# One program order with per-item copy engines for a fused attention and mixing kernel, in place of a greedy order

## Chip, cores and metric

One NeuronCore of a Trainium2 chip. The metric is device time in microseconds (us) of one execution. Most executions of one kernel agree closely (the kernel before: 231.13 to 231.94 us in four); each has a mean granted TensorE clock and a state (fast or slow), and only fast runs are compared.

## The reference, cut to what matters

```python
# attention inside chunks of 64 tokens; B=8, H=8, S=576, D=64
scores = q_c @ k_c.T / sqrt(D);  attn = softmax(scores);  x = attn @ v_c
# mixing, per batch; x: [576, 512]
theta = x @ w_theta                       # 512 x 512
y = w_tok_r @ (x*cos(theta)) + w_tok_i @ (x*sin(theta))   # 576 x 576 each
u = x + y
out = u + relu(u @ w_ch)
```

## The kernel before

The eight batches are worked on in four pairs `p`. A pair has nine tiles of 128 tokens in five groups `g`; group 2 is the middle tile, half of it from each batch. The steps of TensorE are: `a1` transposes q and k, `a2` scores, `a3` attention times v, `a4` transposes x, `a5` theta, `tw` transposes the token weights, `y` mixes tokens, `w` is the last product. Each takes one of four buffers in PSUM (where this kernel's matmuls write), and copies on VectorE (DVE) or ScalarE (ACT) free it. The copies are called by what they write: qT, kT and xT are q, k and x transposed; `sin` and `cos` come from theta. Everything is emitted in program order, for each engine its own instructions.

```python
psum = ctx.enter_context(tc.tile_pool(name="psum", bufs=4, space=bass.MemoryType.PSUM))
def psum2(name, dtype=FP32):              # every step takes one of these four
    n = 1024 if dtype == FP32 else 2048
    return psum.tile([P, n], dtype, name=name, tag="ps")

def a1(p, g):
    ps = psum2("ps_qkT", FP16)
    ...                                   # 32 transposes
    nc.vector.tensor_copy(out=qT[...], in_=psv[:, 0, ...])
    nc.scalar.copy(out=kT[...].rearrange("p e s t -> p e t s"), in_=psv[:, 1, ...])

def a4(p, g):
    ...                                   # 4 transposes per tile
    if n == 2:
        nc.scalar.copy(out=xT[...], in_=psv)
        return
    nc.scalar.copy(out=xm, in_=psv)       # the middle tile
    for bb in range(2):
        nc.gpsimd.tensor_copy(out=xT[:, :, bb*S + KT*P : (bb+1)*S], in_=xm[:, :, bb*CH : bb*CH + CH])

# order: a greedy list scheduler with estimated durations picks the next step
od.segment([], front(0, B0) + tws + back(0, B0))          # B0 = groups 0, 2, 1
for p in range(NP):
    ...
    od.segment(main, back(p, B1), tail=4.0)               # main: y and w
    od.flush()
    if more:
        new_pair(p + 1)
        load_batch(p + 1, B0 + B1)                        # loads, issued from GpSimd
    ...
```

The softmax here doesn't subtract the row's maximum and nothing guards it: scores larger than these inputs give would overflow.

## Time and profile before

| | before |
|---|---|
| timed runs, median (range), 3 runs | 231.5 us (231.13 to 231.94) |
| the profiled run | 228.7 us, span 226.9, granted clock 0.995 |
| TensorE / VectorE / ScalarE / GpSimd busy | 201.7 / 120.2 / 130.5 / 88.5 us |
| first `ps_y` matmul starts; last matmul ends | 33.5; 222.6 us |

The lines behind this are in the prediction. In the rows of 40 slices a digit is a tenth of a slice's time. In a list of waits, "A <- B: 2.4, 3, 0.8" means that A waited 2.4 us in all, three times, at most 0.8, and that B came last. "issue" as a releaser means that the profile shows nothing that was waited for.

### The profile page before, as it was taken

The numbers are of one execution on the slowest core, as the hardware profiler recorded it, in microseconds if no ns is written. First come the engines' busy times: TensorE is split into PE (matmuls) and PEld (weight loads), VectorE is DVE, ScalarE is ACT, GpSimd is POOL, SyncE is SP. The second block draws the span as 40 slices with busy tenths as digits, with TensorE's granted clock in tenths as the row PEclk, the third lists the DMA queues.
The fourth block names the chain that finished last, engine by engine and source line by source line (L and its number), as shares of the span: only waits on it lengthen the run. The fifth ranks groups of instructions, "written<-read, shape, count | busy, mean of one in ns | idle before, by whom it ended". The sixth has DMA issues, their size and how long they took to land.

```text
span 226.9 us, 6743 instructions
## 1 busy us (share of the span) xinstructions
PE 201.7 (89%) x2994; PEld 140.3 (62%) x2994; DVE 120.2 (53%) x214; ACT 130.5 (58%) x151; POOL 88.5 (39%) x124
## 2 busy tenths in 40 slices
PE   0678979997898998999898998999898998999992
PEld 0564567855676656766785656666785657667751
DVE  0135373825547478446446477446456477356353
ACT  2355968357885881167785880267785880364142
POOL 8995487499100195981000295971000200000000
PEclk9999999999999999999999999999999999999998
DMA  6999999999920179999400189999200124013036
GB/s 63 165 156 186 192 180 187 144 124 168 222 22 3 48 102 197 221 168 208 129 3 3 49 118 225 195 169 222 99 3 3 49 69 139 3 46 139 2 110 217
DMA packets 83581, 26.93 MB, mean 119 GB/s; under 512 B 76256, under 2 KB 78944, under 8 KB 83552
## 3 DMA queue, kind: packets, MB, share of 16 engines
q0 software_dynamic: 77664, 16.54, 82.3%
q1 hardware_dynamic: 5888, 9.96, 12.6%
q8 instruction: 23, 0.38, 0.7%
q14 instruction: 6, 0.05, 0.1%
HBM read 33.06 MB, written 9.44 MB: 187 GB/s over the span
## 4 chain that ended last, share of the span: by engine, by line
PE 75%; ACT 14%; DVE 6%; DMA 2%; issue 1%; POOL 0%; DVEq 0%; ACTq 0%; POOLq 0%
PE ps_y L476 32%; PE ps_uw L496 13%; PE ps_theta L420 13%; ACT eT L342 5%; PE ps_qkT L307 5%; PE ps_sT L335 3%; PE ps_uw L503 3%; DMA qk<-in_k_dram 2%; PE ps_xT L391 2%; DVE uT L484 2%; DVE x L377 2%; ACT kT L317 2%; ACT cos L430 2%; ACT xT L398 2%; PE ps_x L363 2%
## 5 line engine op out<-in xcount | busy, mean ns | idle before, releaser
L476 PE MATMUL ps_y<-wT,z 128*128 128x288 f16 x512 | 68.2, 286 | 4.5 <-DVE x L377 2.4
L476 PEld LDWEIGHTS <-z 128*128 128x128 f16 x512 | 48.6, 98 | 18.5 <-DVE x L377 2.7
L246 POOL DMA_DIRECT2D v<-in_v_dram x56 | 42.1, 776 | 14.6 <-DMA qk<-in_k_dram 9.2
L484 DVE TENSOR_TENSOR uT<-ps_y,xT 128x576 f16<-128x576 f32 x32 | 24.2, 758 | 40.0 <-PE ps_y L476 40.0
L496 PE MATMUL ps_uw<-wch,uT 128*128 128x512 f16 x144 | 41.0, 379 | 2.3 <-ACT xT L398 1.7
L317 ACT COPY kT<-ps_qkT 128x1024 f16<-128x1024 f16 (+1 forms) x20 | 23.4, 1193 | 17.9 <-DVE qT L316 17.9
L404 POOL COPY xT<-xTm 128x256 f16<-128x256 f16 x8 | 4.9, 652 | 72.3 <-ACT xTm L402 72.3
L420 PE MATMUL ps_theta<-wtheta,xT 128*128 128x512 f16 x128 | 31.2, 388 | 1.7 <-ACT xT L398 1.7
L430 ACT ACTIVATE cos<-ps_theta,pihalf 128x1024 f16<-128x1024 f32 (+1 forms) x20 | 20.6, 1030 | 19.8 <-PE ps_theta L420 19.8
L503 PE MATMUL ps_uw<-id,uT 128*128 128x128 f16 x144 | 31.5, 219 | 0.0
L509 ACT ACTIVATE relu<-ps_uw 128x512 f32<-128x512 f32 x36 | 20.8, 603 | 18.4 <-PE ps_uw L503 18.4
L398 ACT COPY xT<-ps_xT 128x1024 f16<-128x1024 f16 x16 | 16.2, 1012 | 23.0 <-PE ps_xT L391 23.0
L515 DVE TENSOR_TENSOR o<-ps_uw,relu 128x512 f32<-128x512 f32 x36 | 24.0, 687 | 7.3 <-ACT relu L509 7.3
L307 PE MATMUL ps_qkT<-id,qk 128*64 128x128 f16 (+1 forms) x640 | 22.1, 227 | 6.4 <-DMA qk<-in_q_dram 5.8
L377 DVE TENSOR_TENSOR x<-ps_x,recip 128x512 f16<-128x512 f32 x36 | 24.9, 692 | 1.2
L307 PEld LDWEIGHTS <-qk 128*64 128x64 f16 (+1 forms) x640 | 18.9, 118 | 9.4 <-DMA qk<-in_q_dram 6.2
L316 DVE COPY qT<-ps_qkT 128x1024 f16<-128x1024 f16 (+1 forms) x20 | 12.6, 636 | 22.7 <-PE ps_qkT L307 22.7
L496 PEld LDWEIGHTS <-uT 128*128 128x128 f16 x144 | 14.1, 98 | 15.8
L420 PEld LDWEIGHTS <-xT 128*128 128x128 f16 x128 | 12.6, 100 | 15.7 <-ACT xT L398 2.1
L342 ACT ACTIVATE eT<-ps_sT 128x1024 f16<-128x1024 f32 (+1 forms) x20 | 18.3, 939 | 7.1 <-PE ps_sT L335 7.0
L443 DVE TENSOR_TENSOR z<-x,cos 128x1024 f16<-128x1024 f16 x16 | 11.1, 691 | 20.6 <-ACT cos L430 20.4
L225 POOL DMA_DIRECT2D qk<-in_k_dram x24 | 19.2, 804 | 3.6 <-DMA wch<-in_moe_w_ch_dram 1.6
(41 smaller groups left out, 199.1 us busy)
## 6 DMA issues: line engine op xcount, KB each, us to landing
out_dram<-o SPq DMA_DIRECT2D x32, 256.0 KB, 3.9
qk<-in_q_dram POOLq DMA_DIRECT2D x16, 256.0 KB, 6.4
qk<-in_k_dram POOLq DMA_DIRECT2D x16, 256.0 KB, 7.4
v<-in_v_dram POOLq DMA_DIRECT2D x40, 64.0 KB, 6.7
v<-in_v_dram POOLq DMA_DIRECT2D x16, 128.0 KB, 6.6
out_dram<-o SPq DMA_DIRECT2D x8, 128.0 KB, 4.1
wnat<-in_moe_w_tok_r_dram POOLq DMA_DIRECT2D x1, 576.0 KB, 9.9
wnat<-in_moe_w_tok_i_dram POOLq DMA_DIRECT2D x1, 576.0 KB, 11.9
```

The source lines that it names most:

```text
L246: nc.gpsimd.dma_start(v16[pp : pp + m, sl, :, 0:D], v[2 * p + bb, :, s0 : s0 + m, :].rearrange("h s d -> s h d"),)
L307: nc.tensor.transpose(psv[par * D : par * D + D, w, e, tk, 0:rows], t[0:rows, w, 2 * e + par, tk, :], id16[0:rows, 0:rows],)
L317: nc.scalar.copy(out=kT[:, :, 0:rows, :].rearrange("p e s t -> p e t s"), in_=psv[:, 1, :, :, 0:rows],)
L342: nc.scalar.activation(out=eT[:, 0:n].rearrange("p i e r c -> p r (i e) c"), in_=psv[:, :, 0:n].rearrange("p r i e c -> p r (i e) c"), fun ...
L377: nc.vector.tensor_tensor(out=xo, in0=px[:, :, :, 0:D], in1=recip.broadcast_to((P, 2, NE, D)), op=ALU.mult,)
L420: nc.tensor.matmul(ps[:, jj * DM : jj * DM + DM], xt[:, db, :], wtheta16[:, db, :], start=(db == 0), stop=(db == NDB - 1),)
L430: nc.scalar.activation(out=cos[:, 0:n].rearrange("p a e -> p (a e)"), in_=pin, func=AF.Sin, bias=pihalf, scale=1.0,)
L476: nc.tensor.matmul(psv[:, hf, 0:HS], z[:, db * P : db * P + P], wT[:, kt, hf * HS : hf * HS + HS], start=(kt == 0), stop=(kt == 2 * KT),)
L484: nc.vector.tensor_tensor(out=s["uT"][:, db, sl].rearrange("p (f c) -> p f c", f=2), in0=psv[:, :, 0:HS], in1=s["xT"][:, db, sl].rearrange ...
L496: nc.tensor.matmul(ps[:, 0:DM], uT[:, db, j * P : j * P + P], wch16[:, db, :], start=(db == 0), stop=(db == NDB - 1),)
L503: nc.tensor.matmul(ps[:, DM + db * P : DM + db * P + P], uT[:, db, j * P : j * P + P], id16,)
L515: nc.vector.tensor_tensor(out=o, in0=ps[:, DM : 2 * DM], in1=r, op=ALU.add)
```

## The change

The intent is to replace the greedy scheduler by a fixed order, found by annealing, that has no stalls on the four PSUM buffers. Each item carries flags for which engine copies. Groups are loaded and used in the order 0 to 4, x is held per group, the token weights come and are transposed in halves, and the middle tile's copy leaves GpSimd. The core of the diff, with cuts:

```diff
+ORDER = """
+a1.0.0:0 a2.0.0:0 a1.0.1:3 a3.0.0.0:0 a3.0.0.1:0 a2.0.1:0 a1.0.2:0 a3.0.1.0:0 a2.0.2:0
+a3.0.2.0:0 a4.0.2:3 a4.0.0:0 a3.0.1.1:0 a5.0.2:0 a4.0.1:1 z.0.2.0:0 a5.0.1:0 a5.0.0:0
+tw.1.2:0 z.0.0.0:0 z.0.0.1:0 tw.0.0:1 z.0.1.0:0 z.0.1.1:0 tw.1.1:1 tw.0.1:0 tw.0.2:0
+tw.1.0:1 a1.0.3:2 yh.0.0:0 a2.0.3:0 yh.0.1:0 ...            (cut)
-class Order: ...                                             (cut: the greedy scheduler)
+    def copy(eng, out, in_):
+        if eng: nc.vector.tensor_copy(out=out, in_=in_)
+        else:   nc.scalar.copy(out=out, in_=in_)
     def a1(p, g, bits):
-        nc.vector.tensor_copy(out=qT[...], in_=psv[:, 0, ...])
-        nc.scalar.copy(out=kT[...], in_=psv[:, 1, ...])
+        copy(not bits & 1, qT[...], psv[:, 0, ...])
+        copy(bits & 2, kT[...], psv[:, 1, ...])
     def a4(p, g, bits):
-        nc.scalar.copy(out=xm, in_=psv)
-        for bb in range(2):
-            nc.gpsimd.tensor_copy(out=xT[...], in_=xm[...])
+        copy(bits & 1, xm, psv)
+        copy(not bits & 2, xT.rearrange("p a (b s) -> p a b s", b=2)[:, :, :, KT*P : S],
+             xm.rearrange("p a (b s) -> p a b s", b=2))
+    # x16: one tile per group, bufs=6; before, one tile per pair, bufs=1
+    for item in ORDER:
+        ...                                # emit the step; then, as soon as a q/k buffer
+        load(loaded)                       # and a v slot are free in this order, the next load
```

## The prediction

> **What bounds the kernel now.** I read the page first (busy shares, the 40 slices, the chain), then the waits of TensorE and GpSimd, then the timeline of TensorE up to the first `ps_y`. From the page of the kernel before:
>
> ```profile
> span 226.9 us, 6743 instructions
> PE 201.7 (89%) x2994; PEld 140.3 (62%) x2994; DVE 120.2 (53%) x214; ACT 130.5 (58%) x151; POOL 88.5 (39%) x124
> ...
> PEclk9999999999999999999999999999999999999998
> DMA  6999999999920179999400189999200124013036
> ...
> PE 75%; ACT 14%; DVE 6%; DMA 2%; issue 1%; POOL 0%; DVEq 0%; ACTq 0%; POOLq 0%
> ```
>
> TensorE is the bound: 75% of the chain that ends last, at a full clock. VectorE and ScalarE are a little over half busy, and DMA works in bursts with long empty slices. But 89% busy is not 89% of what TensorE could do, so I count slots instead: how far one step's start lies from the next when nothing waits. These pieces of the chain in order of time (start, duration, what) give them:
>
> ```profile
> 89.09 0.25 PE ps_x L363 x16
> ...
> 91.66 0.45 PE ps_xT L391 x8
> ...
> 105.11 1.01 PE ps_qkT L307 x32
> ...
> 195.76 1.73 PE ps_theta L420 x8
> ...
> 206.21 6.62 PE ps_y L476 x54
> ```
>
> So `y` (18 matmuls) costs 6.62/3 = 2.21 us, 8 theta matmuls 1.73, 32 transposes of q and k 1.01, 8 of x 0.45, 16 attention matmuls 0.25. From the same views: scores 0.62 per 32, a small group's 32 transposes 0.63, `w` 1.08 (four pairs, 0.27 apart), 15 weight transposes 1.01. Whole kernel: y 32 x 2.21 = 70.7; w 36 x 1.08 = 38.9; theta 144 x 0.216 = 31.1; q and k 16 x 1.01 + 4 x 0.63 = 18.7; scores 18 x 0.62 = 11.2; attention 36 x 0.25 = 9.0; x 18 x 0.45 = 8.1; weights 50 x 0.067 = 3.4. Sum 191.1 us. The first matmul starts at 5.8 and the last ends at 222.6, 4.3 before the end (relu 0.60, add 0.69, store). So 216.8 - 191.1 = 25.7 us are lost between them. The first `ps_y` starts at 33.5; the work ahead of it is 15.3 us, so 33.5 - 5.8 - 15.3 = **12.4 us are lost in the opening** and (222.6 - 33.5) - 175.8 = **13.3 us after it**.
>
> TensorE's waits (line, releaser, us in total, times, longest) name them in part; the rest is restarts and stretches inside busy records:
>
> ```profile
> PE ps_y L476 <- DVE x L377: 2.4, 3, 0.8
> PE ps_sT L335 <- ACT kT L317: 2.1, 2, 1.1
> PE ps_uw L496 <- ACT xT L398: 1.7, 3, 0.6
> PE ps_theta L420 <- ACT xT L398: 1.7, 1, 1.7
> PE ps_y L476 <- ACT eT L342: 1.7, 2, 0.8
> ```
>
> `ps_y` needs neither `x` nor `eT` of the next group: it waits for one of the four PSUM buffers, freed by the copy named. So the steady loss is order: several short steps in a row, each leaving a copy of about 1 us, use up four buffers. GpSimd's waits:
>
> ```profile
> POOL xT L404 <- ACT xTm L402: 72.3, 3, 25.7
> ```
>
> The copies of the middle tile stand in the queue that issues the loads and hold it three times for some 25 us. After the first y no TensorE wait names a load, though, so this is hidden.
>
> [...] a `ps_y` matmul has a record of 286 ns but a slot of 2.21/18 = 123 ns. [...] the qT copy, 1024 elements, takes 690 ns, barely more than the 512-element f32 multiply's 692. The change puts kT, written at step 2, on VectorE, where no record of before exists[...]. [...]
>
> **The change part by part.** (1) *Matmuls.* I set the built order of both kernels side by side: the same 5990 rows on TensorE. The first batch's y is cut at 256 and 320 columns instead of 288 twice, the same total. No work goes; the floor stays 191.1. (2) *Table loads.* 10 before and 10 after: 0. (3) *Middle tile.* Eight GpSimd copies (4.9 us) go, four copies come: three on VectorE, one on ScalarE, below 0.6 us each. Off the path; what it buys is that loads are issued as the seven q/k buffers come free. (4) *Copies split.* Counting the order's flags: 9 kT move from ScalarE to VectorE, 6 qT the other way, about half of the xT copies to VectorE. ScalarE loses about 9 x 1.3 + 10 x 1.0 and gains 6 x 1.0: 130 to about 115. VectorE gains about 9 x 1.2 + 10 x 0.7 - 6 x 0.7: 120 to about 133. Both stay near 60%, below TensorE: worth time only where a buffer waited for the busier of the two. (5) *Opening.* Groups go 0, 1, 2, and the token weights are loaded and transposed in halves, but the order puts all six transposing steps ahead of the first y, and the first of them needs the last weight tail. In the trace that tail lands at about 27.8 (issued 16.7, 11.1 to landing); ScalarE then still has sin to 29.2 and three wT copies, two of 1280 elements. Walked by hand with these durations, the last wT copy y needs ends near 32.3 and the first y starts near 32.7: **0.8 us gained**, not the 12.4. (6) *Order after the opening.* The next pair's attention is spread thinly between y and w and x is held per group (six buffers). Walking the stretch from pair 0's `w` into its second half[...], every buffer is free at or just before its turn, with slack of 0.2 to 0.7 us. A real run won't hold that everywhere. My choice: **of the 13.3 us, 4.5 remain, 8.8 gained.** Sum: 0.8 + 8.8 = 9.6 us; span 226.9 - 9.6 = 217.3. The timed runs are 231.5 for a span of 226.9; I take the same microseconds off: **221.9, say 222.0 us**, 4.1% less.
>
> **The rivals.** *Loads become the bound.* Pairs 2 and 3 are transposed much earlier: by summed slots plus the opening, pair 2's first group at about 68 us and pair 3's at about 97, against 105 and 156 before. GpSimd issues a full group in 4.1 us (12.2 us for three from 45.2 to 57.4), landing about 7 later, so pair 2's group 0 lands near 65 and pair 1's group 1 near 47 against a need near 48.7. Slack is 2 to 4 us, and stores run beside it. If loads lag, TensorE stands 2 to 6 us between 45 and 80 us: 224 to 228. For it: slices at 9 in DMA up to 60 us. Against it: every delay elsewhere adds slack. *Four buffers still bind.* The slack of the walk is used up by longer copies (kT at 1.2 us)[...], so that 8 to 10 us stay: about 226. For it: PSUM still has four buffers and every step's copies are about as long. *The opening worsens*, by 1 to 3 us, because the weights come in six transfers instead of four and the first transposing step waits for the last of them, in front of everything: 223 to 225. *Everything holds*: 1 to 2 us lost after the opening, 218.5 to 219.5. [...]
>
> **Range and chances.** Gain if all holds 13, centre 9.6, with one rival 4 to 6, with two about 2. So 218.5 to 227.5 holds it 8 times in 10. Faster by over 2% means below 226.9: it needs only 4.6 of the 25.7 us; 0.85. Within 2%: two rivals together, 0.13. Slower: only if an order tuned to a model meets a load it did not foresee, 0.02.
>
> **What would show each step.** TensorE's sum of slots unchanged and its busy time lower than 201.7 by a few us (fewer restarts). The first `ps_y` at 32 to 33.5; if at 30 or at 35, step 5 is wrong. GpSimd never waiting for xTm, and the DMA row without its empty slices up to about 110 us. VectorE near 133 and ScalarE near 115 us busy, kT on VectorE near 1.2 us. Between the first y and the last matmul about 180 us instead of 189. A TensorE wait on q, k or v after 40 us would mean the first rival; a few us on VectorE or ScalarE copies ahead of y, w or the short steps, the second. The prediction is wrong above all if the 4.5 us is: nothing in the trace of before measures it.

## More of the kernel before

One line pair of the kernel before that I had looked at but not used is TensorE's timeline at its first theta (start, duration, engine, line, operation, how many):

```profile
21.38 2.85 PE L420 MATMUL ps_theta<-wtheta,xT 128*128 128x512 f16 x8
24.07 1.03 PE L420 MATMUL ps_theta<-wtheta,xTm 128*128 128x512 f16 x4
24.94 1.89 PE L420 MATMUL ps_theta<-wtheta,xT 128*128 128x512 f16 x8
```

The first eight matmuls take 24.07 - 21.38 = 2.7 us up to the next start, the last eight 1.7.

## The result, and the profile after

A ratio is the mean time of one kernel's fast runs over that of the other's of the same rounds, so it is not quite the ratio of the medians.

| | median (range), runs | ratio to before, 95% interval |
|---|---|---|
| before | 231.63 us (231.13 to 231.94), 4 | 1 |
| changed | 224.76 us (223.36 to 228.51), 4, one of them slow | 0.9685 (0.9623 to 0.9748) |
| changed (`after_again`) | 222.92 us (222.14 to 223.81), 4 | 0.9637 (0.9575 to 0.970) |

So it is 3.1 to 3.6% faster; 4.1% was predicted. The profile that came with the result fell in the slow state (clock 0.982), so I read `after_again`, the same kernel in the fast state. From its page:

```profile
span 221.7 us, 6717 instructions
PE 200.3 (90%) x2994; PEld 139.2 (63%) x2994; DVE 130.7 (59%) x230; ACT 117.4 (53%) x136; POOL 85.1 (38%) x118
...
PEclk9999999999999999999999999999999999999999
DMA  5999999999999999999990012112211211321236
...
PE 79%; DMA 10%; POOL 5%; issue 2%; ACT 1%; DVE 1%; ACTq 0%; POOLq 0%
```

The matmuls are the same 2994, VectorE and ScalarE have changed places, and the empty DMA slices before 115 us are gone. TensorE's waits after 45 us:

```profile
PE ps_sT L292 <- issue: 1.7, 2, 1.0
PE ps_sT L292 <- ACT kT L199: 0.6, 1, 0.6
PE ps_x L320 <- issue: 0.4, 1, 0.4
```

Of the list of before nothing is left but 0.6 us on one copy. In its place stand waits on nothing visible. Now the opening, from TensorE's timeline of the same run:

```profile
22.89 1.89 PE L377 MATMUL ps_theta<-wtheta,xTm 128*128 128x512 f16 x4
26.41 5.37 PE L377 MATMUL ps_theta<-wtheta,xT 128*128 128x512 f16 x16 [0.79 <-DVE xT L197]
...
37.09 1.05 PE L434 MATMUL ps_y<-wT,z 128*128 128x256 f16 x8
```

The first `ps_y` starts at 37.1, where before it started at 33.5. From there to the end of the last matmul it is 180.3 us instead of 189.1. So the part after the first y gained 8.8 us, and the opening lost 3.6.

There is a third term. The kernel before had granted clocks of 0.968 to 0.988 in the 25 runs timed beside the experiments, against 0.995 in its profiled run; all fast runs of the changed kernel had 0.996 to 1.000. The profiled run of before took 228.7 us, some 3 us less than its timed runs. So some 3 us of the timed difference seem to come with the clock, beside 5.2 us of span (226.9 to 221.7); that the clock is the reason was not shown.

### The profile page after: what moved, and what is told of

It is laid out like the page before. It is cut to its first block, busy times and chain, and to the rows that moved or that the text cites.

```text
span 226.4 us, 6717 instructions
## 1 busy us (share of the span) xinstructions
PE 203.6 (90%) x2994; PEld 140.9 (62%) x2994; DVE 130.9 (58%) x230; ACT 117.3 (52%) x136; POOL 85.1 (38%) x118
## 4 chain that ended last, share of the span: by engine, by line
PE 83%; ACT 6%; DVE 4%; issue 2%; DMA 2%; POOL 0%; ACTq 0%; POOLq 0%
PE ps_y L455 27%; PE ps_theta L377 16%; PE ps_uw L475 14%; PE ps_qkT L266 8%; PE ps_y L434 4%; PE ps_sT L292 4%; PE ps_xT L348 4%; PE ps_uw L482 4%; PE ps_x L320 3%; DMA qk<-in_k_dram 2%; ACT kT L199 2%; ACT eT L299 2%; DVE x L334 1%; DVE kT L197 1%; DVE qT L197 1%
## 5 line engine op out<-in xcount | busy, mean ns | idle before, releaser
L455 PE MATMUL ps_y<-wT,z 128*128 128x288 f16 x448 | 60.4, 289 | 0.0
L455 PEld LDWEIGHTS <-z 128*128 128x128 f16 x448 | 42.9, 99 | 13.3 <-issue 0.3
L475 PE MATMUL ps_uw<-wch,uT 128*128 128x512 f16 x144 | 43.5, 386 | 0.0
L463 DVE TENSOR_TENSOR uT<-ps_y,xT 128x576 f16<-128x576 f32 x28 | 21.2, 756 | 28.1 <-PE ps_y L455 28.0
L377 PE MATMUL ps_theta<-wtheta,xT 128*128 128x512 f16 x128 | 32.3, 400 | 0.8 <-DVE xT L197 0.8
L199 ACT COPY kT<-ps_qkT 128x1024 f16<-128x1024 f16 (+1 forms) x11 | 12.6, 1146 | 20.5 <-DVE qT L197 20.4
L155 POOL DMA_DIRECT2D qk<-in_q_dram x24 | 19.4, 813 | 1.4 <-POOLq L558 0.8
L391 ACT ACTIVATE sin<-ps_theta 128x1024 f16<-128x1024 f32 (+1 forms) x20 | 18.7, 935 | 0.0
L292 PE MATMUL ps_sT<-qT,kT 64*64 64x64 f16 x576 | 13.1, 224 | 5.2 <-ACT kT L199 3.3
L320 PE MATMUL ps_x<-v,eT 64*64 64x65 f16 x576 | 11.8, 202 | 4.1 <-issue 1.7
```

Of the source, the lines that this page charges most:

```text
L155: nc.gpsimd.dma_start(t[(pp // 2) : (pp // 2) + m // 2, ti].rearrange("p h t d -> p h (t d)"), src.rearrange("h (p t) d -> p h (t d)", t=2),)
L292: nc.tensor.matmul(psv[kh * CH : kh * CH + CH, par, i, e, :], kT[par * D : par * D + D, e, c0 : c0 + CH], qT[par * D : par * D + D, e, c0 ...
L377: nc.tensor.matmul(ps[:, jj * DM : jj * DM + DM], xt[:, db, :], wtheta16[:, db, :], start=(db == 0), stop=(db == NDB - 1),)
L455: nc.tensor.matmul(psv[:, hf, 0:HS], zt[:, db * P : db * P + P], wT[:, kt, hf * HS : hf * HS + HS], start=(kt == 0), stop=(kt == 2 * KT),)
L475: nc.tensor.matmul(ps[:, 0:DM], uT[:, db, j * P : j * P + P], wch16[:, db, :], start=(db == 0), stop=(db == NDB - 1),)
```

## The experiments

Twelve kernels ran.

**1. `after_again`: the changed kernel, unchanged.**

> The changed kernel unchanged, for a profile in the fast state. Both theories: 223 to 225.5 us, first ps_y at 36 to 37.5 us, theta matmuls in the opening at about 0.43 us from start to start (half speed) as in the first profile, and from the first y to the last matmul about 180 us. If the slow state alone had made the late opening, the first ps_y is here at 34 or below.

Measured: 222.92 us, first y at 37.1, 180.3 us after it.

**2. `open_before`: the opening put back.**

```diff
-a1.0.0:0 a2.0.0:0 a1.0.1:3 a3.0.0.0:0 ... a4.0.1:1 z.0.2.0:0 a5.0.1:0 a5.0.0:0
+a1.0.0:0 a1.0.2:0 a2.0.0:0 a2.0.2:0 a1.0.1:0 a3.0.0.0:0 a2.0.1:0 a3.0.0.1:0 a3.0.2.0:0
+a4.0.0:0 a3.0.1.0:0 a4.0.2:0 a3.0.1.1:0 a4.0.1:0 a5.0.0:0 a5.0.2:0 a5.0.1:0 z.0.2.0:0
+    LOADS[1], LOADS[2] = LOADS[2], LOADS[1]
```

> The changed kernel with the opening of pair 0 put back to the kernel before: loads and steps in the order 0, 2, 1 and no split of copies there, all that follows unchanged. Theory A (the new opening is a longer chain: two big groups first, qT on ScalarE and then kT on VectorE, and TensorE has more gaps): first ps_y at 33 to 34 us, total down 3 to 4 us, about 220.5. Rival B (the weights in six transfers instead of four delay the opening): first ps_y stays at 36 to 37, total within 1 us of the changed kernel.

Measured: first y at 33.6, as theory A expects, with the weights still in six transfers, so rival B falls. But the total is 222.33 us, only 0.6 below `after_again` (0.9 by the fast runs alone; one of its four was slow): a miss of some 3 us. From the first y to the last matmul it took 182.2 us instead of 180.3. The waits of this run that name no releaser:

```profile
PE ps_sT L292 <- issue: 3.0, 2, 1.8
...
PE ps_x L320 <- issue: 0.8, 1, 0.8
```

**3. `warm`: throw-away work in TensorE's gaps of the opening.**

```diff
+    warm = const.tile([P, 512], FP16, name="warm");  nc.vector.memset(warm, 0.5)
+    # into the PSUM buffer just taken, ahead of the step's own matmuls:
+    #   9 before the first step, 6 before a2.0.0, 5 before a3.0.0.0, 1 to 3 at five others,
+    #   10 transposes before a4.0.2
+    nc.tensor.matmul(ps[:, 0:512], warm[:, 0:P], warm)
```

> The changed kernel with throw-away matmuls and transposes in TensorE's gaps of the opening, written into the PSUM buffer of the next step ahead of its own work (results unchanged). Theory C [...]: theta matmuls in the opening at 0.22 us instead of 0.43, first ps_y at about 34, total down about 3 us. Theory A alone: theta slots get shorter but the chain of copies sets the first ps_y, at 36 or later, total down less than 1 us. If throw-away work does not speed TensorE up, slots stay at 0.43 and the total rises by up to 1 us.

The opening looks as theory C says:

```profile
22.68 1.04 PE L391 MATMUL ps_theta<-wtheta,xTm 128*128 128x512 f16 x4
...
25.09 3.63 PE L391 MATMUL ps_theta<-wtheta,xT 128*128 128x512 f16 x16
...
34.07 1.05 PE L448 MATMUL ps_y<-wT,z 128*128 128x256 f16 x8
```

Sixteen matmuls take 3.63 us instead of 5.37, and the first y starts at 34.1 instead of 37.1. Start to start they are 216 ns apart; in `after_again` they are 427 ns apart until 29.8 us and 216 from 30.1 on. One trace doesn't show that the throw-away work did it, though: `after_3`, `nosplit` and `pool_mid` have the changed kernel's opening without it, and their sixteen also ran at some 216 ns (first y at 35.0, 35.4 and 35.0). What only `warm` has is the short time in the first four too (1.04 us, in `after_again` 1.89); all five traces of this opening without throw-away work show those at 401 to 427 ns from start to start. Yet the total is 224.15 us, above `after_again`, with intervals that overlap. Again the part after the first y grew, to 182.7 us.

**4. `pool_mid`: the middle tile's copies back on GpSimd.** (The edit is the a4 part of the diff above, reversed.)

> The changed kernel with the middle tile's copies back on GpSimd. If in this order they stand behind the loads issued ahead of them (pair 1's first five groups, issued until about 55 us), pair 0's middle columns come only then, the additions of the first batch's second half wait, and the total rises by 8 to 15 us, to 232 to 239. If the move off GpSimd is worth nothing, within 1 us of the changed kernel.

Measured: 238.73 us, 15.8 more than `after_again` on the same chip. VectorE's longest wait after the first y, and TensorE's:

```profile
DVE uT L442 <- POOL xT L361: 15.1, 1, 15.1
...
PE ps_x L320 <- DVE uT L442: 11.6, 1, 11.6
```

The copies ran at 58.1 us, behind all loads issued ahead of them, and pair 0's first additions waited. Of the 15.8 us some 3 are more stops of the kind that comes next (6.0 us against 2.7). In this order the move off GpSimd is necessary, though in the old one it was worth nothing (experiment 5).

**What stops TensorE.** In experiments 1 to 3, TensorE stands in the middle of steps, where nothing is waited for. I numbered its records in the trace (weight loads, matmuls and its few sequencer records, in order of start, from 0). In `after_again` the gaps are before numbers 2241, 2753 and 3777; in `warm`, whose throw-away work shifts all numbers by 78, before 2241, 2497, 2753, 3009, 3777 and 4033. All are 193 modulo 256. The DMA part of the page has the other half:

```profile
q8 instruction: 23, 0.38, 0.7%
```

These are 23 packets of 16,384 bytes. If these 0.38 MB are the program of TensorE's 5990 instructions, one has some 63 bytes and a packet holds some 260: an estimate from these numbers, near the 256 of the gaps. The number of packets follows TensorE's instructions: 21 in `few_rows` with 5342, 24 in `warm` with 78 more. Ahead of each such gap one of them starts 2.2 to 2.8 us before TensorE goes on. So the reading is: TensorE has used up its program and waits for the next packet. Experiments 7, 9 and 12 test it. In the next table "stops" is the sum of the gaps over 0.4 us at these numbers, start to start, and the rest is what is left of the time from the first y to the end of the last matmul.

| kernel | first y | first y to last matmul | stops (how many) | rest |
|---|---|---|---|---|
| before | 33.5 | 189.1 | 0 | 189.1 |
| after_again | 37.1 | 180.3 | 2.7 (3) | 177.6 |
| after_3 | 35.0 | 180.8 | 3.2 (3) | 177.6 |
| open_before | 33.6 | 182.2 | 4.4 (3) | 177.8 |
| open_before_2 | 33.6 | 182.4 | 2.4 (2) | 180.0 |
| warm | 34.1 | 182.7 | 5.3 (6) | 177.4 |
| open_warm | 33.6 | 184.1 | 6.5 (5) | 177.6 |
| open_no_late_v | 34.1 | 183.2 | 4.8 (3) | 178.4 |
| few_rows | 34.1 | 178.3 | 0 | 178.3 |
| open_spread | 33.3 | 181.0 | 3.1 (3) | 177.9 |
| nosplit | 35.4 | 187.5 | 4.1 (3) | 183.4 |
| before_mid | 34.5 | 192.1 | 2.7 (2) | 189.4 |
| pool_mid | 35.0 | 198.1 | 6.0 (3) | 192.1 |

For nearly all kernels with the new order the rest is 177.4 to 178.4 us, against a floor of 175.8 by summed slots. The exception, `open_before_2`, had a granted clock of 0.93 between 66 and 90 us, right where its stops are.

**5. `before_mid`: the kernel before with one part of the change.** (Its a4 copies the middle tile with one `nc.vector.tensor_copy`.)

> The kernel before with one part of the change alone: the middle tile's copies on VectorE in one instruction instead of two on GpSimd, so that loads are no longer held up. If the loads are hidden in the old order, the time stays within 1 us of the kernel before although GpSimd never waits for xTm. If loads held it back, 2 us or more faster.

Measured: 233.41 us, ratio 1.0083 (1.0009 to 1.0157). GpSimd now waits for a free q/k buffer instead of for xTm:

```profile
POOL qk L225 <- PE ps_qkT L307: 15.7, 1, 15.7
```

The loads were hidden; this part alone gains nothing in the old order. The extra 1.3 us fit the two stops in its profile (which also has a granted clock of 0.50 from 32 to 36 us, in the opening); why they came here and not in the kernel before is answered under experiment 7.

**6. `nosplit`: every copy after the opening on its old engine, order unchanged.**

```diff
-tw.1.0:1 a1.0.3:2 yh.0.0:0 a2.0.3:0 yh.0.1:0 a1.0.4:2 ...   a4.0.4:1 ...
+tw.1.0:1 a1.0.3:0 yh.0.0:0 a2.0.3:0 yh.0.1:0 a1.0.4:0 ...   a4.0.4:0 ...
```

> The changed kernel with the split of the copies undone after the opening: qT on VectorE, kT and xT on ScalarE for every item, order unchanged. If the split matters because the four PSUM buffers are freed by whichever engine is less loaded, TensorE's waits on ScalarE copies grow and the total rises by 3 to 6 us. If the order alone does it, within 1 us.

Measured: 229.19 us, ratio to before 0.9878, where the changed kernel has 0.9637 and 0.9645: some 5.5 us. The rest column says the same, 183.4 instead of 177.6. TensorE's waits after 45 us show them coming back, apart from the stops:

```profile
PE ps_theta L377 <- ACT sin L391: 0.9, 1, 0.9
PE ps_uw L475 <- ACT sin L391: 0.9, 2, 0.6
PE ps_qkT L266 <- DVE o L494: 0.9, 1, 0.9
PE ps_xT L348 <- DVE o L494: 0.6, 1, 0.6
```

These steps don't read `sin` or `o`; they wait for the buffer that the reader held. The order was tuned together with the split, so 5.5 us is what the split is worth in this order, not a share that would add up.

**7. `open_no_late_v`: open_before without v's loads of pairs 2 and 3 (wrong values).**

```diff
     def load_v(p, g):
+        if p >= 2:
+            return
```

> open_before without the loads of v for pairs 2 and 3 (their results are wrong on purpose: old v is used). In open_before TensorE stands three times for 4.4 us in all in the middle of a step, waiting for nothing but its program; each stop is at an instruction number of 193 modulo 256[...]. If the program arrives late because the loads fill the DMA engines, with far fewer load packets between 60 and 105 us the first two stops shrink from 3.0 to under 1 us and the total falls by 2 us or more. If the stops come from how fast TensorE uses up instructions, they stay at 3 to 4.5 us, and the total within 1 us.

Measured: 224.32 us, stops of 4.8 us. That looks as if the theory "program late because loads fill the DMA engines" fell, but the run didn't empty the DMA engines where its three stops are. With v's loads gone, GpSimd issued those of q and k earlier. From TensorE's entry into each of the three stretches of 256 before these stops to the start of the next packet, `--windows` gives a DMA share of 1.55, 1.83 and 1.80, against 1.89, 1.95 and 1.35 in `open_before`. (The share sums the packets' times, so packets that overlap take it over 1.) Where the loads really were gone, the stop is gone too: the last load packet ended at 93.4 us instead of 115.1, and the stop before 3777 is missing. In `after_again`, too, that stop ends at 116.3 us, while load packets were under way until 116.6. Two pairs of traces show what loads do. In each pair TensorE takes the same time over the same stretch of 256 instructions:

| stretch ends before | kernel | load packets under way when the next program packet starts | it starts, us into the stretch | stretch takes | stop after it |
|---|---|---|---|---|---|
| 3777 | open_before | 34 | 3.8 | 4.8 | 1.4 |
| 3777 | open_no_late_v | 0 | 0.8 | 4.8 | 0 |
| 3521 | before_mid | 32 | 3.3 | 4.8 | 1.1 |
| 3521 | before | 0 | 0.1 | 4.8 | 0 |

The second pair in wider windows, first `before`, then `before_mid` (the last two numbers of a line are the DMA share and GB/s):

```profile
115.00:130.00 15.00, 14.08 (x291) 10.33 (x290) 8.97 (x17) 11.18 (x12) 1.02 (x2) 1.00 0.06 21
120.00:123.00 3.00, 2.91 (x62) 1.00 2.14 166
```

So a stop is what the packet's late start and the 2.2 to 2.8 us that follow it exceed the stretch by: 3.8 + 2.4 - 4.8 = 1.4. After the first y, over all 14 traces, the next packet started at most 1.4 us into the stretch when no load packet was under way at its start (136 packets), and 2.7 in the median, at most 4.8, when one was (143). Of the 38 stops, 36 came with loads under way; the two before 4033 in `warm` and `open_warm` came without, after stretches of 2.7 and 2.8 us. So both terms count, how fast TensorE uses up its program and how long loads hold up the next packet. This also answers experiment 5: with GpSimd no longer held up, the loads ran beside these stretches. The other stop of `before_mid`, before 1985, is of the same kind: the packet started 2.7 us into a stretch of 3.7, in `before` 1.0 into one of 3.6.

**8. `open_warm`: open_before with throw-away work.** (The edit of 3, with fewer pieces, on top of 2.)

> open_before with throw-away work in TensorE's gaps of the opening. Theta at full speed from its start: first ps_y at 32 to 32.5 us instead of 33.6. If what is won in the opening is kept, total 1 to 1.5 us below open_before. If it is given back where TensorE waits for its program in the dense stretch from 70 to 90 us, the same total and more of those stops.

Measured: 223.81 us and five stops of 6.5 us. The first y stayed at 33.6: theta ended earlier, but TensorE then waited for the token weights:

```profile
28.28 1.79 PE L232 MATMUL ps_wT<-id,wnat 128*64 128x128 f16 x25 [0.95 <-DMA wnat<-in_moe_w_tok_i_dram]
```

So in the old opening the landing of the weights and the copies after it set the first y, not theta's speed: its last eight matmuls started at 25.26 us instead of 25.86, and the y at 33.6 in both.

**9. `few_rows`: open_before with less TensorE program (wrong values).**

```diff
+                    if p >= 1:
+                        if h4 == 0:       # one head's weights for four heads
+                            nc.tensor.matmul(psv[..., 0 : NE*(D+1)], eT[...], v16[..., h : h+NE, 0 : D+1])
+                        continue
```

> open_before with 648 fewer TensorE instructions (5342 rows of program instead of 5990): in pairs 1 to 3 an attention step uses one head's weights for four heads, 4 matmuls of 260 columns instead of 16 of 65 (wrong values on purpose, the same columns, waits and copies). If TensorE is short of program in the dense stretches, its stops at program packets fall from 3 to 6 us to under 1.5 us and the total is 2.5 to 5 us below open_before. If the stops have another cause, they stay and the total is within 1 us of open_before.

Measured: 218.54 us, 3.3 below `open_before_2` in the same rounds, with no stop. The stretch that ends before 2241 takes 7.2 us instead of 4.8, so a packet that starts 3.5 us into it is in time. (With q and k drawn as small as the reference draws them, all attention weights of a chunk should be nearly equal.) All of TensorE's waits after 45 us:

```profile
PE ps_sT L292 <- ACT kT L199: 0.6, 1, 0.6
PE ps_qkT L266 <- ACT kT L199: 0.5, 1, 0.5
PE ps_uw L483 <- ACT kT L199: 0.3, 1, 0.3
```

The six timed runs lie within 0.46 us (218.21 to 218.67) at a clock of 0.999 or more, while `open_before_2` had clocks of 0.972 to 0.997 and the changed kernel in the same rounds ran from 221.47 to 225.63. A link between stops and clock is not shown by this: the profiled run of `after_again` had three stops and a clock of 0.999.

**10 and 11. `after_3` and `open_before_2`: the two again, in five rounds on one chip.**

> The changed kernel again, on the chip and in the rounds of the three below, as their measure: 222.5 to 225.5 us.

> open_before again with more rounds. If the opening's gain of 3.5 us is really given back to stops for program, it is within 1 us of the changed kernel; if the first comparison was only noisy, 2 to 3.5 us below it.

Measured: `after_3` 224.08 us, ratio to before 0.9645 (0.9596 to 0.9694); `open_before_2` 221.87 us, 0.9588 (0.9554 to 0.9621). The gap is 0.6% by the ratios, 1.3 us, between the two forecasts (within 1 us, or 2 to 3.5): of the 1.4 us that the opening is earlier in these two profiles about as much is kept, but the intervals overlap. The opening of `after_3` differed from `after_again`'s although the kernel is the same:

```profile
26.01 3.63 PE L377 MATMUL ps_theta<-wtheta,xT 128*128 128x512 f16 x16 [0.79 <-DVE xT L197]
...
34.99 1.05 PE L434 MATMUL ps_y<-wT,z 128*128 128x256 f16 x8
```

Here theta ran at some 216 ns from start to start from 26.0 us, and y started 2.1 us earlier. So 2.1 of the 3.6 us that the opening lost go with theta at 427 ns, which comes or not from run to run (in two of five traces of this opening), and some 1.5 with the longer chain.

**12. `open_spread`: open_before with one score step moved out of the densest stretch, and the attention step that needs it behind it; results right.**

```diff
-... a1.2.2:0 a3.1.4.1:0 a2.2.1:0 a4.1.1:1 z.1.0.1:0 w.0.4:0 ... w.0.5:0 st.0.5:0 a3.2.1.0:0 a1.2.3:2 a5.1.2:0 w.0.6:0 ...
+... a1.2.2:0 a3.1.4.1:0 a4.1.1:1 z.1.0.1:0 w.0.4:0 ... w.0.5:0 st.0.5:0 a2.2.1:0 a1.2.3:2 a5.1.2:0 w.0.6:0 a3.2.1.0:0 ...
```

> open_before with one score step of pair 2 (64 rows of program) taken out of the densest stretch and put four steps later, results right. Stretches of 256 rows there last 4.6, 4.65 and 4.5 us by summed slots; the third becomes 6.8. If stops come where several such stretches follow each other in under 5 us each, the stop near 82 us (1 to 2.5 us) goes and the total falls by about 1 to 1.5 us against open_before. If not, the stop stays, or the total is the same.

Measured: 220.34 us (219.59 to 220.88), ratio to before 0.953 (0.950 to 0.956), 1.5 us below `open_before_2`. The gap before 2753, near 82 us, is gone; three others are there, 3.1 us in all, and the one before 4033 (1.2 us) is new. So the stop went where it was expected to, but the sum of stops is no smaller than in `open_before_2` (2.4), and that the 1.5 us come from it isn't shown. This is the fastest kernel here with right results, ahead of the changed kernel of the same rounds with intervals apart.

## Why the prediction was right or wrong

- **Bound and floor: right.** TensorE stays the bound, with the same matmuls; rest after the first y 177.6 against a slot sum of 175.8.
- **"Of the 13.3 us, 4.5 remain": right in size, wrong in content.** 180.3 - 175.8 = 4.5 us remained in `after_again` (5.0 in `after_3`). But I put it down to the schedule's lost slack. In truth the PSUM waits are all but gone (1.8 us with restarts), and 2.7 us are stops for program, which I had in no rival. That the size agrees is luck.
- **The opening: wrong, and the step that failed is part 5**, "Walked by hand with these durations ... the first y starts near 32.7". It came at 37.1 and 35.0. Two terms were mis-sized. First, I walked theta at 1.73 us per eight; in the opening it takes up to 3.4 (427 ns from start to start in `after_again`, later 216). In the trace of before and in the changed kernel's first one the slots fall from 427 to 216 ns within 0.2 us of the start of the first clock record (23.3 and 30.6 us). Ahead of it there is none, and the row of granted clock reads 9 there all the same. What brings the step was not shown. The trace of before showed the slow slots, 2.7 us for the first eight theta, and I took the slot from the warm part all the same. Second, the chain: qT on ScalarE and then kT on VectorE, one after the other, delay the second group, and the x transposes start at 21.0 instead of 17.0. `open_before` gives the opening back (33.6), with the order of groups and the flags together, so their shares aren't separated.
- **Middle tile, "Off the path": wrong.** I checked the old order and the old path. In the new order the old copies would cost 15.8 us (`pool_mid`); in the old order the new copies gain nothing (`before_mid`). A part's worth depends on the order around it.
- **Copies split: right in loads, too low in worth.** ScalarE 117.4 (said 115), VectorE 130.7 (133), kT on VectorE 1.30 us (1.2 was my estimate; the trace of before has no kT on VectorE); but without the split 5.5 us are lost, more than half of the 8.8 gained after the first y (by the rest column 5.8 of 11.5). One slip in the prediction: it calls qT's 690 ns "barely more than" 692, and it is just under.

The two forms of kT in `after_again` (line, engine, operation, shapes, count | busy, mean ns | idle before, releaser):

```profile
L199 ACT COPY kT<-ps_qkT 128x1024 f16<-128x1024 f16 x8 | 10.4, 1305 | 15.0 <-DVE qT L197 15.0
L197 DVE COPY kT<-ps_qkT 128x1024 f16<-128x1024 f16 x8 | 10.4, 1299 | 7.3 <-ACT qT L199 7.3
```

- **Rivals.** Loads as the bound: not as forecast; after 37 us no TensorE wait of `after_again` names a load. But loads do cost by a path that no rival had: the next program packet starts later beside them (experiment 7: 2.7 us into the stretch in the median, at most 1.4 without). Buffers still binding: no, 0.6 us. The opening worsening: yes, by 3.6 us instead of the 1 to 3, and not for the reason given: with the same six transfers `open_before` has the old start.
- **The clock: missed.** I took the span's difference over to the timed runs one to one. The span fell by 5.2 us instead of 9.6; the timed medians fell by 6.9 to 9.0, it seems because before had a lower granted clock in its timed runs than in its profiled one. Part of the agreement with 222.0 is therefore luck.

What stays open: how TensorE's next packet is asked for and why loads hold it up (no run thinned out the loads alone beside every dense stretch), and where the timed runs of the kernel before lose clock.

## What to carry to other kernels

Once buffers and copies are in balance, look at what a wait on "issue" in the middle of a step hides: count the instructions per microsecond of the bounding engine and look which loads run beside it, because here short matmuls used up program faster than it arrived, nearly always while loads were under way (36 of 38 stops): in `open_before` TensorE took 4.8 us over 256 instructions, the next packet started 3.8 us into them among 34 load packets, and TensorE stood 1.4 us. Time won ahead of a dense stretch can then be given back inside it. And before an experiment counts against a theory, check that it changed what it was meant to change: `open_no_late_v` took loads away, but not where the stops were. Walk an opening with the slots of the opening, not with those of the steady part. Test each part of a change in the new order and in the old one: a copy that was off the path in one cost 15.8 us in the other.
